# A gated pair of spectral filters: the first inverse step mostly without column tiles, rows of x and the last output row in smaller pieces

## The chip, the core and the metric

The kernel runs on one core of one Trainium2 chip. The metric is the device time of one launch in microseconds (us). Before the change the median of three runs is 131.76 us (131.26 to 131.91). One further execution was profiled, and the views below are of that one.

## What is computed

One input x of 2048 rows and 1024 columns goes through two filters in the frequency domain (a two-dimensional real transform, a product with complex weights, the inverse transform). A gate, one number per row of x, mixes the two results. Both filters get the same x, so the forward transform is made once. Only A_x is read; B_x is not used by the reference either.

```python
def _A_ref(x, w_r, w_i):            # _B_ref is the same function
    B, S, D = x.shape               # 1, 2048, 1024, bfloat16
    X = jnp.fft.rfft2(x.astype(jnp.float32), axes=(-2, -1))
    X = X * (w_r + 1j * w_i)        # weights (2048, 513)
    y = jnp.fft.irfft2(X, s=(S, D), axes=(-2, -1)).astype(jnp.bfloat16)
    return y

x = A_x
g = sigmoid((x * gate_w).sum(-1, keepdims=True))
a = _A_ref(x, A_w_r, A_w_i)
b = _B_ref(x, B_w_r, B_w_i)
return g * a + (1 - g) * b
```

## The kernel before

The transforms are matrix products. A row of the input has two numbers: its place p on the 128 partitions and n2, one of 16, so that n2 counts 16 "row blocks" of 128 rows. The stages, by the names of the planner's nodes:

- **x, F, W, DM, SK, DI, MS, RM**: loads on SP's queue. xload (line 544) brings two row blocks (512 KB) at a time, DEPTH and FP give the order of x and of the parts of the matrix F. W0 and W1 are the weights of the two filters, four times four parts each. DM is loaded a second time at the end with other contents (RM).
- **fS, fT** (lines 632, 633): VectorE folds two row blocks, sum and difference of each row with its mirror image; for block 14 another pair (u0, u1) follows. **S1**: eight matmuls for each row block; **Z**: its eviction from PSUM to R3.
- **gate, zrow, zg, zp**: four groups of matmuls with 32 columns of the array for each (line 616), for the gate's transform.
- **D, Q** and **S2, X** for 16 groups kg: the rest of the forward transform, eight 256-wide matmuls and two tiny ones, then four 512-wide ones, each with an eviction of 128 x 1024.
- **mul, sum** (prod, line 729): VectorE multiplies X with the weights of filter b, for the pair m of two groups kg, in two products of 2048 elements and two sums of 1024. The pairs in SPLIT leave the sums out, and the matmuls behind them have twice the terms ("wide").
- **I1, V, turn** (stage_i1, line 751): the first inverse step. For each filter b, pair m and half h, each matmul has 64 weight columns and writes 64 PSUM partitions; r = 0 and r = 1 sit beside each other in the array as two column tiles. So one group is eight matmuls (sixteen when wide), one eviction V of 128 x 1024 into a "ub" tile, and one transfer "turn" of 256 KB within the on-chip memory, from the 128 partitions of ub to 16 partitions of U, eight rows of 2 KB in each (lines 777 to 779). There are 32 such groups, 16 for each filter.
- **x5, p5m, p5a, v5, V5, v5t, U5**: the last frequency column, 512, by itself. **gm, sig, RA, RB**: the gate and its product with the second inverse matrix.
- **Sj0, Sj1, Sk1, T, Dinv, o** (inverse, line 854): for each row block the second inverse step, eight matmuls for each filter into one PSUM tile (Sk1, the one that needs U5, stands alone), an eviction T, eight matmuls Dinv and an eviction o. Block n2 needs all turns with h = n2 // 8. Then **h0, h1, y0, y1** on VectorE and the transfer **out**; two row blocks share these except the last two, 14 and 15, which have them alone.

The order within each engine is planned: TABLE holds, for each node in the order in which the program adds it, a letter for its engine (p TensorE, a ScalarE, v VectorE, s SP) and a number, its place. Plan.run (line 321) walks through the nodes as an event simulation with costs written by hand; on each engine, the node of lowest place that is ready and finds room in its tile pools goes next. The pools and their limits are in the Plan at line 481 ("ub": ten tiles between V and the landing of the turn). The result is a fixed instruction order for each engine, with semaphores. All helpers record at a few lines: L493 is every matmul, L496 every VectorE operation on two tensors, L518 an eviction by ScalarE, L519 an eviction by VectorE, L524 every transfer.

Of the kernel before, what the change touches and what calls it, by code (L numbers as in the profile page):

```python
# [9 lines left out]
ALU = mybir.AluOpType  # L10
AP = bass.AP
# [6 lines left out]
v80 a100 s90 s145 s200 s255 s310 s365 s420 s475 s530 s585 s640 s695 a240 s750 s805 s860 s915 s978 s1105 s1168 s1295  # L18
s1358 s1421 s1484 s1548 s1611 s1674 s1737 s1801 s1864 s1927 s1990 s2054 v90 p160 a612 p1815 a1862 v505 v444 p666
v774 p578 a712 v611 v672 p840 a953 p753 a861 v888 v948 p1022 a1130 p1109 a1222 v1088 v1028 p1284 a1405 p1197 a1313  # L20
v1305 v1244 p1378 a1496 p1466 a1588 v1379 v1439 p1640 a1771 p1553 a1679 v1513 v1573 p1728 a1869 p1839 v1947 v1708
v1648 v1782 v1855 p1970 a2039 p2070 a2135 p1926 a1991 p2058 p2014 v2091 p2166 p2114 v2199 p2288 p2245 a2321 p2393
v2426 p2508 v2532 s2109 s2172 s2298 s2362 s2488 s2551 s2615 s2678 s2741 s2804 s2868 s2931 s2994 s3057 s3121 s3184
p2300 a2414 p2523 a2631 p2414 a2529 p2703 v2810 v3052 v3226 v2939 v3166 p3501 a3636 s3745 p3328 a3453 s3562 p2610
a2724 p2883 a2995 p2789 a2904 p3062 a3178 v3288 v3515 v3401 v3575 p3767 a3910 s4020 p3681 a3819 s3928 p2969 a3087
p3242 a3361 p3149 a3270 p3415 a3544 v4096 v4270 v3983 v4210 p4477 a4642 s4752 p4387 a4551 s4660 p3587 a3727 p3853
a4002 p3940 a4093 p4206 a4368 v4792 v5019 v4905 v5079 p5372 a5509 s5618 p5192 a5326 s5435 p4294 a4459 p4569 v4678
p4660 a4774 p4933 a5051 v5487 v5714 v5600 v5774 p5897 a6009 s6119 p5983 a6101 s6210 p4840 a4960 p5106 a5234 p5278
a5417 p5551 a5692 v6062 v6235 v5948 v6175 p6737 a6870 s6979 p6478 a6595 s6705 p5458 a5600 p5724 v5834 p6069 a6192
p6391 a6504 v6870 v6997 v7057 v7184 p7353 a7466 s7575 p7439 a7557 s7666 p6184 a6298 p6650 a6778 p6298 a6412 p6564  # L30
a6687 v7258 v7372 p7698 a7892 s8001 p7526 a7719 s7829 v6984 p7168 v7245 v7833 v7846 v8467 v8477 v8533 v8520 v8559
# [14 lines left out]
QD = False  # L46
SPLIT = ((0, 7), (1, 6), (1, 7))
FULL = (14,)
DEPTH = tuple((i, i + 2) for i in range(0, 16, 2))
FP = ((0, 2), (2, 6), (6, 11), (11, 16))  # L50


# [888 lines left out]
```

## Time and profile before

| | us |
|---|---|
| median of the runs | 131.76 |
| the profiled execution | 131.37 |
| its span in the profile | 129.5 |
| TensorE busy | 117.5 |
| VectorE busy | 107.5 |
| ScalarE busy | 100.2 |

The span is the time from the first to the last instruction of the profiled execution; 1.9 us of its time lie outside. PE is TensorE's matmuls, PEld its weight loads, DVE VectorE, ACT ScalarE, SP the engine that issues transfers. A row of the table by stretch has the stretch, its length, then the busy time of each engine with the number of instructions, the granted clock of TensorE, the share of time in which the 16 DMA engines were busy, and the rate. A row of the timeline has the start, the length, the engine, the line and operation, output <- input with the names of the on-chip tensors (PS is PSUM, R the large buffers, RING the tile ring), the shape, how many were merged, and in brackets the idle time before and what ended it. "128*64 128x512" is a matmul with 128 rows and 64 columns of the array and 512 elements streamed. The ends of matmuls are modelled and overlap, so that their starts tell more than their busy time.

### The profile page before, as it was taken

The page shows a single profiled execution, that of the slowest core. Times are in us where ns is not written, and L with a number is a line of the kernel's source. Part 1 is how long each engine was busy: PE and PEld are TensorE (multiplying, and loading weights), DVE is VectorE, ACT ScalarE, POOL GpSimd, SP SyncE. Part 2 cuts the span into 40 slices and gives each one's busy share as a digit, 9 for nine tenths or more (in the row PEclk, how much of TensorE's full clock was granted, in tenths as well). Part 3 has the DMA queues.
Part 4 walks back from the last instruction along what each step waited for, and adds up shares of the span by engine and source line. Part 5 has one row for each costly group of instructions (what it writes and reads, how often), then busy time and mean ns, then how long its engine had stood idle before and what let it go on. Part 6 is the DMA issues. An engine that isn't in the chain of part 4 may idle for free.

```text
span 129.5 us, 2793 instructions
## 1 busy us (share of the span) xinstructions
PE 117.5 (91%) x1149; PEld 76.6 (59%) x1149; DVE 107.5 (83%) x155; ACT 100.2 (77%) x109; POOL 0.2 (0%) x4
## 2 busy tenths in 40 slices
PE   6687999899999999999999999999969999999710
PEld 2365786566544455445483555555659999999600
DVE  1386796417999997998899999998965899999992
ACT  4348898597999997999799958667335659999950
POOL 0000000000000000000000000000000000000000
PEclk9999999999999999999999999999999999999996
DMA  4999999999999997406348998987630004435474
GB/s 116 289 379 419 407 418 372 378 378 387 382 380 372 218 193 180 132 0 161 90 128 217 289 209 190 221 200 168 172 81 5 0 0 167 162 149 197 173 297 162
DMA packets 14064, 28.62 MB, mean 221 GB/s; under 512 B 1506, under 2 KB 5858, under 8 KB 14051
## 3 DMA queue, kind: packets, MB, share of 16 engines
q1 hardware_dynamic: 14048, 28.44, 70.2%
q8 instruction: 9, 0.15, 0.5%
q14 instruction: 5, 0.03, 0.1%
q10 hardware_dynamic: 2, 0.00, 0.0%
HBM read 15.85 MB, written 4.19 MB: 155 GB/s over the span
## 4 chain that ended last, share of the span: by engine, by line
PE 60%; DVE 20%; DMA 9%; issue 3%; SPq 3%; ACT 2%; DVEq 0%
PE PS L493 60%; DVE R L496 14%; DMA R<-in_A_x_dram 7%; DVE R L519 4%; SPq L524 3%; DMA R<-RING 3%; ACT R L518 2%; DVE RING L496 1%; DVE RING L519 1%; ACT RING L518 1%; DVEq L248 0%; DVE V L519 0%
## 5 line engine op out<-in xcount | busy, mean ns | idle before, releaser
L518 ACT ACTIVATE R<-PS 128x1024 bf16<-128x1024 f32 x52 | 50.9, 1028 | 12.9 <-PE PS L493 12.7
L518 ACT ACTIVATE RING<-PS 128x1024 bf16<-128x1024 f32 (+1 forms) x48 | 46.7, 1008 | 8.8 <-PE PS L493 8.8
L496 DVE TENSOR_TENSOR RING<-R 128x2048 bf16<-128x2048 bf16 (+1 forms) x48 | 47.8, 1043 | 6.2 <-DMA R<-in_A_x_dram 6.1
L493 PE MATMUL PS<-RING,SK 128*64 128x512 bf16 (+1 forms) x368 | 51.2, 382 | 0.1
L493 PEld LDWEIGHTS PS<-RING,SK 128*64 128x64 bf16 (+1 forms) x368 | 21.5, 108 | 24.3 <-issue 6.7
L493 PE MATMUL PS<-DM,R 128*128 128x256 bf16 (+1 forms) x256 | 27.4, 245 | 0.5 <-DMA R<-RING 0.5
L493 PEld LDWEIGHTS PS<-DM,R 128*128 128x128 bf16 x256 | 18.9, 97 | 5.7 <-issue 2.1
L519 DVE CAST R<-PS 128x1024 bf16<-128x1024 f32 (+1 forms) x16 | 15.2, 961 | 8.1 <-PE PS L493 8.1
L496 DVE TENSOR_TENSOR R<-R 128x1024 bf16<-128x1024 bf16 (+1 forms) x36 | 20.6, 626 | 0.3
L496 DVE TENSOR_TENSOR RING<-RING 128x1024 bf16<-128x1024 bf16 x28 | 18.2, 684 | 0.1
L493 PE MATMUL PS<-DI,R 128*128 128x256 bf16 x128 | 16.1, 273 | 1.3 <-ACT R L518 1.3
L493 PE MATMUL PS<-R,RING 128*128 128x256 bf16 (+1 forms) x128 | 14.5, 266 | 2.6 <-DVE RING L496 2.6
L493 PEld LDWEIGHTS PS<-R,RING 128*128 128x128 bf16 x128 | 11.4, 98 | 6.0 <-DVE RING L496 4.5
L493 PEld LDWEIGHTS PS<-DI,R 128*128 128x128 bf16 x128 | 11.7, 98 | 3.0 <-ACT R L518 1.6
L493 PE MATMUL PS<-RING,R 128*128 128x128 bf16 x128 | 9.3, 219 | 0.0
L493 PEld LDWEIGHTS PS<-RING,R 128*128 128x128 bf16 x128 | 7.7, 98 | 0.6 <-DVE R L519 0.4
L493 PE MATMUL PS<-MS,R 128*128 128x1 bf16 (+1 forms) x40 | 5.2, 165 | 0.0
L519 DVE CAST RING<-PS 128x512 bf16<-128x512 f32 (+1 forms) x4 | 3.8, 958 | 1.6 <-PE PS L493 1.5
L493 PE MATMUL PS<-RING 128*128 128x512 bf16 x8 | 3.5, 615 | 1.2 <-DVE RING L588 1.2
L493 PEld LDWEIGHTS PS<-MS,R 128*128 128x128 bf16 (+1 forms) x40 | 3.4, 96 | 0.4 <-issue 0.2
L844 ACT ACTIVATE RING<-PS 128x512 bf16<-128x512 f32 x4 | 2.4, 601 | 1.1 <-DVE RING L496 1.1
L493 PE MATMUL PS<-R,G 128*32 128x512 bf16 x32 | 2.5, 384 | 0.4 <-ACT R L518 0.4
(34 smaller groups left out, 17.7 us busy)
## 6 DMA issues: line engine op xcount, KB each, us to landing
R<-RING SPq DMA_DIRECT2D x32, 256.0 KB, 4.4
R<-in_A_x_dram SPq DMA_DIRECT2D x8, 512.0 KB, 8.3
out_dram<-R SPq DMA_DIRECT2D x7, 512.0 KB, 2.6
R<-in_A_w_r_dram SPq DMA_DIRECT2D x7, 256.5 KB, 9.6
R<-in_A_w_i_dram SPq DMA_DIRECT2D x7, 256.5 KB, 9.5
R<-in_B_w_i_dram SPq DMA_DIRECT2D x7, 256.5 KB, 8.1
R<-in_B_w_r_dram SPq DMA_DIRECT2D x7, 256.5 KB, 8.2
R<-c_F SPq DMA_DIRECT2D x2, 320.0 KB, 7.6
```

The source lines that it names most:

```text
L493: return lambda e: e.matmul(o, l, r, start=start, stop=stop, skip_group_check=True)
L496: return lambda e: e.tensor_tensor(out=o, in0=a, in1=b, op=op)
L518: return [lambda e: e.activation(o, i, ACT.Copy)]
L519: return [lambda e: e.tensor_copy(o, i)]
L524: lambda e: [lambda q, d=d, s=s: q.dma_start(d, s) for d, s in pairs()],
L844: P.add("sig", {"act": (0.5, 0.7)}, lambda e: [lambda e: e.activation(rg(gr, 0, [[1, 512]]), psl(t, 0, [[1, 512]]), ACT.Sigmoid)], [(t,)], ...
```

## The change

- Of the 16 pairs (b, m), all but (1,5), (1,6) and (1,7) lose the column tiles. Each r has a group of its own (I0): four matmuls (eight when wide) of 128 weight columns, which give both halves h for one group kg. Its eviction is 128 x 1024 as before, and it is turned by two transfers of 128 KB: 64 source partitions of ub to 8 partitions of U, for h = 0 and h = 1. The three tiled pairs keep one transfer for each h. Keys of U now count 16 groups kg instead of eight pairs.
- x is loaded as single row blocks for 0, 1, 14 and 15, with pairs between; F comes in three parts instead of four. The folds of blocks 0 to 3 and 14, 15 are made in single row blocks, four operations of 512 for two blocks instead of two of 1024.
- The warm-up has seven matmuls instead of eight.
- Sk1 is merged into Sj1 where n2 % 8 > 1.
- For the last row block, Dinv, eviction (oh), h0 and h1 are made in two halves (by parity of the column frequency), and the output goes out as two transfers of 128 KB, one behind y1 and one behind y0.
- The planner gets a cost for going into or out of a tiled shape on TensorE, other pool limits, a rate of 400 instead of 390 for x, and a new TABLE. By the new table the four gate groups stand together, the wide group of (1,7) is split by v5 and v5t, the gate mix (gm, sig, RA, RB) comes before the last V, and VectorE gets the evictions X1, Q7, V of (1,3) and V of (1,6) between 27 and 88 us of the table's places (before: X1, X8, X12 and both V of (1,4)).

The diff without the table:

```diff
@@ -15,39 +15,42 @@
 NW = 16 * NS
 CELL = 512
...
 QD = False
 SPLIT = ((0, 7), (1, 6), (1, 7))
+TILED = ((1, 5), (1, 6), (1, 7))
 FULL = (14,)
-DEPTH = tuple((i, i + 2) for i in range(0, 16, 2))
-FP = ((0, 2), (2, 6), (6, 11), (11, 16))
+DEPTH = ((0, 1), (1, 2)) + tuple((i, i + 2) for i in range(2, 14, 2)) + ((14, 15), (15, 16))
+FP = {1: (0, 4), 3: (4, 8), 5: (8, 16)}
...
+        self.switch = 0.11
...
+                    if e == "pe" and n.kind != kind:
+                        kind = n.kind
+                        occ, lat = occ + self.switch, lat + self.switch
                     n.eng, n.start = e, now
                     free[e] = now + occ
                     n.end = now + lat
@@ -479,9 +486,9 @@
     GW = R4
 
     P = Plan({"ps": 8, "ring": NCELL, "t": 32, "late": 32},
-             {"ps": ("ps", 4), "p1": ("ps", 8), "sj": ("ps", 3), "st": ("ring", 3), "u": ("ring", 1), "q": ("ring", 4),
-              "t": ("ring", 2), "tn": ("ring", 4), "pp": ("ring", 2), "g": ("ring", 1), "gz": ("ring", 1), "RA": ("ring", 1), "ub": ("ring", 10), "w": ("ring", 1), "T": ("t", 4),
-              "o": ("late", 2), "h": ("late", 2), "y": ("late", 3)})
+             {"ps": ("ps", 4), "p1": ("ps", 8), "sj": ("ps", 3), "st": ("ring", 3), "u": ("ring", 2), "q": ("ring", 3),
+              "t": ("ring", 2), "tn": ("ring", 4), "pp": ("ring", 4), "g": ("ring", 2), "gz": ("ring", 2), "RA": ("ring", 1), "ub": ("ring", 10), "w": ("ring", 1), "T": ("t", 3),
+              "o": ("late", 3), "h": ("late", 2), "y": ("late", 3), "yl": ("late", 2)})
     HOME = {"ring": RING, "t": R4, "late": R5}
     xv = A_x[0].rearrange("(p r) d -> p r d", r=16)
     outv = out[0].rearrange("(p r) d -> p r d", r=16)
@@ -503,7 +510,9 @@
         return {"dve": (0.07 + 0.00052 * n, 0.205 + 0.00052 * n)}
 
     def pe(name, ns, build, reads, writes, alloc=(), **kw):
-        return P.add(name, cost(ns), lambda e: build(), reads, writes, alloc=alloc, **kw)
+        n = P.add(name, cost(ns), lambda e: build(), reads, writes, alloc=alloc, **kw)
+        n.kind = {"I1": 1, "gate": 2}.get(name, 0)
+        return n
 
     def ev(name, n, io, reads, writes, slow=False, only=None, **kw):
         x = 0.285 if slow else 0.0
@@ -543,14 +552,12 @@
 
     def xload(a, b):
         dma("x", "sp", lambda: [(ap(R1, a * 1024, [[1024, b - a], [1, 1024]]), xv[:, a:b, :])],
-            (b - a) * 0.262, 390, [], [("x", i) for i in range(a, b)])
-
...
+    for i, (a, b) in enumerate(DEPTH):
+        if i in FP:
+            f0, f1 = FP[i]
+            cload("sp", R2, f0 * 256, "F", f0 * 256, f1 * 256, [("F", j) for j in range(f0, f1)])
         xload(a, b)
     dma("gw", "act", lambda: [(ap(GW, 0, [[1, 1024]], 0, 1), gate_w.rearrange("(o d) -> o d", o=1))], 0.002, 400, [], ["gw"])
     cload("sp", MS, 0, "MS", 0, 410, ["MS"])
@@ -588,7 +595,7 @@
     P.add("zero", {"dve": (0.6, 0.7)}, lambda e: [lambda e: e.memset(rg(warm, 0, [[1, 512]]), 0.0)],
           [], [(warm, 0, 1)], alloc=[warm])
     wps = Tile("p1", 1)
-    pe("warm", [512] * 16, lambda: [mm(psl(wps, 0, [[1, 512]]), rg(warm, 0, [[1, 128]]), rg(warm, 0, [[1, 512]]), True, True) for _ in range(8)],
+    pe("warm", [512] * 14, lambda: [mm(psl(wps, 0, [[1, 512]]), rg(warm, 0, [[1, 128]]), rg(warm, 0, [[1, 512]]), True, True) for _ in range(7)],
        [(warm, 0, 1)], [(wps,)], alloc=[wps])
 
     gp = Tile("p1", 1)
@@ -629,8 +636,15 @@
         lo = ap(R1, n2 * 1024, [[1024, 2], [512, 2], [1, 256]])
         hi = ap(R1, n2 * 1024 + 1023, [[1024, 2], [-512, 2], [-1, 256]])
         xs = [("x", n2), ("x", n2 + 1)]
-        P.add("fS", vt(1024), lambda e: [tt(rg(st, 0, [[1024, 2], [256, 2], [1, 256]]), lo, hi, ALU.add)], xs, [(st, 0, 1), (st, 2, 3)], alloc=[st])
-        P.add("fT", vt(1024), lambda e: [tt(rg(st, 512, [[1024, 2], [256, 2], [1, 256]]), lo, hi, ALU.subtract)], xs, [(st, 1, 2), (st, 3, 4)])
+        if n2 < 4 or n2 == 14:
+            for r in range(2):
+                for name, c, op in (("fS", 0, ALU.add), ("fT", 1, ALU.subtract)):
+                    P.add(name, vt(512), lambda e, r=r, c=c, op=op: [
+                        tt(rg(st, r * 1024 + c * 512, [[256, 2], [1, 256]]), ap(R1, (n2 + r) * 1024, [[512, 2], [1, 256]]),
+                           ap(R1, (n2 + r) * 1024 + 1023, [[-512, 2], [-1, 256]]), op)], xs[r:r + 1], [(st, 2 * r + c, 2 * r + c + 1)], alloc=[st])
+        else:
+            P.add("fS", vt(1024), lambda e: [tt(rg(st, 0, [[1024, 2], [256, 2], [1, 256]]), lo, hi, ALU.add)], xs, [(st, 0, 1), (st, 2, 3)], alloc=[st])
+            P.add("fT", vt(1024), lambda e: [tt(rg(st, 512, [[1024, 2], [256, 2], [1, 256]]), lo, hi, ALU.subtract)], xs, [(st, 1, 2), (st, 3, 4)])
         if n2 not in FULL:
             for r in range(2):
                 stage_s1(n2 + r, st, r)
@@ -752,31 +766,44 @@
         p = PT[b, m]
         T = UR[b]
         pt = pit[id(T)]
-        for h in range(2):
-            P.key = ("IA", "IB")[b], 2 * m + h
+        wide = isinstance(p, list)
+        terms = [(768, 0, 0), (1792, 0, 512), (1024, 1, 0), (1024, 1, 512)] if wide else [(768, 0, 0), (1024, 0, 512)]
+
+        def data(r, i):
+            return rg(p[terms[i][1]] if wide else p, r * 1024 + terms[i][2], [[1, 512]])
+
+        def matrix(r, i, o, w):
+            return ap(SK, terms[i][0] + (512 if r == m == 0 else 0) + o, [[1, w]])
+
+        def turn(u, kgs, h, p0, n, k):
+            dma("turn", "sp", lambda: [(AP(T, (64 * (kgs[0] % 2) + m) * pt + h * 8192, [[8 * pt, k], [1024, 8], [1, 1024]]), rg(u, 0, [[1, 1024]], p0, n))],
+                n / 128 * 0.262, 205, [(u, 0, 2)], [("U", b, kg, h) for kg in kgs], n=1.15, after=allz(h) if b else [("x", i) for i in range(16)])
+
+        if (b, m) in TILED:
+            for h in range(2):
+                P.key = ("IA", "IB")[b], 2 * m + h
+                t, u = Tile("ps", 2), Tile("ub", 2)
+
+                def halves(h=h, t=t):
+                    return [mm(psl(t, o * 512, [[1, 512]], 64 * r, 64), matrix(r, i, o * 128 + h * 64, 64), data(r, i), i == 0, i == len(terms) - 1)
+                            for o in range(2) for i in range(len(terms)) for r in range(2)]
+                keys = [(q, 0, 4) for q in p] if wide else [(p, i, i + 1) for i in range(4)]
+                pe("I1", [512] * 2 * len(terms), halves, keys + ["SK"], [(t,)])
+                ev("V", 1024, lambda t=t, u=u: (rg(u, 0, [[1, 1024]]), psl(t, 0, [[1, 1024]])), [(t,)], [(u, 0, 2)])
+                turn(u, (2 * m, 2 * m + 1), h, 0, 128, 16)
+            return
+        for r in range(2):
+            P.key = ("IA", "IB")[b], 2 * m + r
             t, u = Tile("ps", 2), Tile("ub", 2)
 
...
+            def whole(r=r, t=t):
+                return [mm(psl(t, o * 512, [[1, 512]]), matrix(r, i, o * 128, 128), data(r, i), i == 0, i == len(terms) - 1)
+                        for o in range(2) for i in range(len(terms))]
+            keys = [(q, 0, 4) for q in p] if wide else [(p, 2 * r, 2 * r + 1), (p, 2 * r + 1, 2 * r + 2)]
+            pe("I0", [512] * 2 * len(terms), whole, keys + ["SK"], [(t,)])
             ev("V", 1024, lambda t=t, u=u: (rg(u, 0, [[1, 1024]]), psl(t, 0, [[1, 1024]])), [(t,)], [(u, 0, 2)])
-            dma("turn", "sp", lambda u=u, h=h: [(AP(T, m * pt + h * 8192, [[8 * pt, 16], [1024, 8], [1, 1024]]), rg(u, 0, [[1, 1024]]))],
-                0.262, 205, [(u, 0, 2)], [("U", b, m, h)], n=1.15, after=allz(h) if b else [("x", i) for i in range(16)])
+            for h in range(2):
+                turn(u, (2 * m + r,), h, 64 * h, 64, 8)
 
     def x512():
         P.key = ("x5", 0)
@@ -818,7 +845,7 @@
         pe("v5t", [16] * 8, tr, [("V5", b), "MS"], [(t2,)])
         for h in range(2):
             ev("U5", 8, lambda h=h: (ap(UR[b], 512 + h * 8192, [[1024, 8]]), psl(t2, h * 8, [[1, 8]])), [(t2,)], [("U5", b, h)], only="dve",
-               after=[("U", b, m, h) for m in range(8)])
+               after=[("U", b, kg, h) for kg in range(16)])
 
     for kg in range(16):
         stage_d(kg)
@@ -851,8 +878,29 @@
     for c in range(4):
         gmix(c)
 
+    def finish(v, o, h):
+        for p in range(2):
+            P.key = ("E", 15)
+            t = Tile("p1", 1)
+            pe("Dinv", [256] * 4, lambda p=p, t=t: [
+                mm(psl(t, c * 256, [[1, 256]]), rg(v, (c * 4 + 2 * p + i) * 128, [[1, 128]]), ap(DI, ((2 * p + i) * 2 + c) * 256, [[1, 256]]), i == 0, i == 1)
+                for c in range(2) for i in range(2)], [(v, 0, 2), "DI"], [(t,)], alloc=[t] + ([] if p else [o]))
+            ev("oh", 512, lambda p=p, t=t: (rg(o, p * 512, [[1, 512]]), psl(t, 0, [[1, 512]])), [(t,)], [(o, p, p + 1)])
+            P.key = ("U", 15)
+            a, b = rg2(o, p * 512, [[1, 256]]), rg2(o, p * 512 + 256, [[1, 256]])
+            P.add("h0", vt(256), lambda e, p=p, a=a, b=b: [tt(rg(h, p * 512, [[1, 256]]), a(), b(), ALU.add)], [(o, p, p + 1)], [(h, p, p + 1)], alloc=[] if p else [h])
+            P.add("h1", vt(256), lambda e, p=p, a=a, b=b: [tt(rg(h, p * 512 + 511, [[-1, 256]]), a(), b(), ALU.subtract)], [(o, p, p + 1)], [(h, p, p + 1)])
+        for i, op in enumerate((ALU.add, ALU.subtract)):
+            y = Tile("yl", 1)
+            P.add("y%d" % i, vt(512), lambda e, y=y, i=i, op=op: [
+                tt(rg(y, 256 * i, [[256 - 512 * i, 2], [1, 256]]), rg(h, 0, [[256, 2], [1, 256]]), rg(h, 512, [[256, 2], [1, 256]]), op)],
+                [(h, 0, 1), (h, 1, 2)], [(y, 0, 1)], alloc=[y])
+            d = outv[:, 15, 256:768] if i else AP(outv.tensor, outv[:, 15, 0:256].offset, [list(outv[:, 15, 0:256].ap[0]), [768, 2], [1, 256]])
+            dma("out", "sp", lambda y=y, d=d: [(d, rg(y, 0, [[1, 512]]))], 0.131, 400, [(y, 0, 1)], [], kind="out", n=0.65)
+
     def inverse(ns):
         k = len(ns)
+        last = ns == (15,)
         o, h, y = Tile("o", 2 * k), Tile("h", 2 * k), Tile("y", 2 * k)
         for r, n2 in enumerate(ns):
             P.key = ("S", n2)
@@ -864,14 +912,19 @@
                            R(n2 * 128), b == 0 and j in (0, 4), b == 1 and j in (3, 4)) for j in js]
             for b in range(2):
                 g = ("RB", n2 // 4) if b else (RA, n2 // 4, n2 // 4 + 1)
-                u = [("U", b, m, n2 // 8) for m in range(8)]
+                u = [("U", b, kg, n2 // 8) for kg in range(16)]
                 if not b:
                     pe("Sj0", [128] * 8, lambda fns=fns: fns(0, range(8)), u + [("U5", 0, n2 // 8), g], [(t,)])
+                    continue
+                if n2 % 8 > 1:
+                    pe("Sj1", [128] * 8, lambda fns=fns: fns(1, (0, 1, 2, 3, 5, 6, 7, 4)), u + [("U5", 1, n2 // 8), g], [(t,)])
                     continue
                 pe("Sj1", [128] * 7, lambda fns=fns: fns(1, (0, 1, 2, 3, 5, 6, 7)), u + [g], [(t,)])
                 pe("Sk1", [128], lambda fns=fns: fns(1, (4,)), [("U5", 1, n2 // 8), g], [(t,)])
             ev("T", 1024, lambda t=t, v=v: (rg(v, 0, [[1, 1024]]), psl(t, 0, [[1, 1024]])), [(t,)], [(v, 0, 2)])
             P.key = ("E", n2)
+            if last:
+                break
 
             def inv(t=t2, v=v):
                 f = []
@@ -884,6 +937,8 @@
                 return f
             pe("Dinv", [256] * 8, inv, [(v, 0, 2), "DI"], [(t2,)], alloc=[t2] + ([o] if r == 0 else []))
             ev("o", 1024, lambda t=t2, r=r: (rg(o, r * 1024, [[1, 1024]]), psl(t, 0, [[1, 1024]])), [(t2,)], [(o, 2 * r, 2 * r + 2)])
+        if last:
+            return finish(v, o, h)
         d2 = [1024, k]
         P.key = ("U", ns[0])
         oc = [(o, 2 * r, 2 * r + 2) for r in range(k)]
```

## The prediction

> **What bounds the kernel now.** I read the busy time by stretch first.
>
> ```profile
> core 0: us, PE busy (x) PEld busy (x) DVE busy (x) ACT busy (x) POOL busy (x), PEclk, DMA share, GB/s
> 35.00:50.00 15.00, 15.00 (x119) 7.58 (x119) 14.11 (x17) 14.62 (x16) 0.00 (x0) 1.00 1.01 278
> 50.00:62.00 12.00, 12.00 (x92) 5.57 (x89) 11.16 (x13) 11.57 (x12) 0.00 (x0) 1.00 0.45 116
> 62.00:76.00 14.00, 14.00 (x121) 7.59 (x122) 13.86 (x16) 12.41 (x15) 0.00 (x0) 1.00 0.74 188
> 76.00:90.00 14.00, 14.00 (x135) 7.34 (x134) 13.54 (x25) 10.06 (x11) 0.00 (x0) 1.00 0.90 195
> ...
> 104.00:126.60 22.60, 18.94 (x246) 17.28 (x244) 22.36 (x37) 18.42 (x20) 0.00 (x0) 1.00 0.41 164
> ```
>
> From 35 to 90 us TensorE never rests, and VectorE has 55 - (14.11 + 11.16 + 13.86 + 13.54) = 2.3 us left; ScalarE has 6.3. From 104 us on VectorE is full. The chain that ended last agrees: it stays on TensorE from 27.01 for 62.93 us and from 103 us mostly on VectorE.
>
> So what TensorE does with its time between 35 and 92 us counts. The timeline shows it matmul by matmul:
>
> ```profile
> 49.30 0.49 PE L493 MATMUL PS<-DM,R 128*128 128x256 bf16 x3
> ...
> 50.32 1.05 PE L493 MATMUL PS<-RING,SK 128*64 128x512 bf16 x8
> 51.30 0.50 PE L493 MATMUL PS<-DM,R 128*128 128x256 bf16 x3
> ...
> 52.24 3.96 PE L493 MATMUL PS<-RING,SK 128*128 128x512 bf16 x24
> ```
>
> Starts are to be read, since the ends overlap. A D stage takes 52.24 - 51.30 = 0.94 us when an S2 follows and 51.30 - 50.32 = 0.98 is one I1 group of eight column-tiled matmuls (four pairs). The D stage before that group takes 50.32 - 49.30 = 1.02. Four full 512-wide matmuls (S2) take 0.87: their weights come at 48.42, the next D matmul at 49.30. So pairs of column tiles cost what full matmuls cost, plus 0.08 us on entering the tiled shape and 0.11 on leaving. The waits of weight loads show the same thing, as idle time that nothing releases:
>
> ```profile
> 46.58 1.44 PEld L493 LDWEIGHTS PS<-RING,SK 128*64 128x64 bf16 x16 [0.21 <-issue]
> 48.42 0.55 PEld L493 LDWEIGHTS PS<-RING,SK 128*128 128x128 bf16 x4 [0.41 <-issue]
> ```
>
> Here two groups take 48.42 - 46.58 = 1.84, eight pairs at 0.216 would be 1.73: 0.11 again, with the entry before it. I take 0.21 us for a visit to the tiled shape, in and out.
>
> **The change, part by part.** The profiled execution took 131.37 us, with a span of 129.5; the sum is made against it. The median of the runs shown is 131.76, so 0.39 is added at the end. From the table I use only each node's engine and the order.
>
> *Column tiles.* Before, TensorE goes into the tiled shape 16 times between 35 and 92 us. By the new order only (1,5), (1,6), (1,7) are tiled, in 4 visits. 12 x 0.21 = **-2.5 us** on the engine that sets this stretch (bounds -2.8, and -1 if the neighbours stop it). The work stays: half as many matmuls of full width, the same evictions.
>
> *What is late next there: VectorE.* It has 2.3 us free. Of 1024-wide evictions it gets four instead of five in this stretch, which frees 1.2 (1221 ns each); four gate-mix operations of 512 that came after the last first-step eviction now come ahead of it (0.42 each alone, but two in a row take 0.76 in the chain, so 0.34 to 0.35 apart: 1.4). So 2.3 + 1.2 - 1.4 = 2.1 against the 2.5 that TensorE gives up: VectorE becomes just as tight. **+0.4** (bounds 0 and 1.5). ScalarE takes one more eviction, 1.0 of its 6.3.
>
> *Turns in two transfers.* 32 transfers of 256 KB become 52 of 128 KB and 6 of 256. Issues on SP take 0.38 to 0.71 us each in the chain, some 0.57 with the pause; from the first half of (0,5) to the last transfer that the first Sj1 needs there are 32 halves, 4 whole and the reload of RM: 37 x 0.57 = 21 us, beside some 29 us of TensorE steps (12 narrow and 2 wide full groups, 6 tiled ones, D, S2, gm, v5, three Sj0, 8 shape changes). SP has room, and what waits behind a turn there is only other turns. The data itself: a whole turn runs at 195 GB/s in the row 76 to 90 above, where the DMA share is 0.90; 0.262 MB / 195 = 1.34 us. **A half is not in the trace.** From below it is 0.67; from above it is what a whole one takes, 1.34, if only half of the 16 DMA engines, or of what they meet in memory, serve it (64 source partitions and 8 destination partitions instead of 128 and 16). With 0.67 the stretch needs 32 x 0.67 + 4 x 1.34 + 1.3 = 28.1 us, plus some 2.5 from issue to landing for the last: 30.6 against 29. I charge **+0.9**, taking 0.67 to 0.70, because the only packets that a split adds are four-byte completions. Each 0.1 us more per half adds 3.2 us, as nothing else covers it: the ten ub tiles fill, then evictions wait, then TensorE.
>
> [...]
>
> *The opening.* Before:
>
> ```profile
> 4.33 1.29 DVE L496 TENSOR_TENSOR RING<-R 128x1024 bf16<-128x1024 bf16 x2 [3.18 <-DMA R<-in_A_x_dram]
> ...
> 5.68 1.81 PE L493 MATMUL PS<-R,RING 128*128 128x256 bf16 x15 [1.01 <-DVE RING L496]
> ```
>
> The first fold waits for two rows of x (512 KB) and lasts 1.29; now it waits for one row and two 512-wide operations (0.34 apart), so S1 starts about 1.1 us earlier. Later loads carry the same bytes, so the last row lands where it did, near 17.3 us; TensorE then has less backlog, but not 1.1 less. I take -0.6. The four gate rows stood apart, four visits to a tiled shape (32 columns); now they stand together, one visit: 3 x 0.2 = -0.6. Together **-1.2** (bounds -2.0, and 0 if the last fold, four operations 0.34 apart instead of two in 1.30, then the u pair, ends as late as before). One warm matmul less lies ahead of the first load's landing and costs nothing unless the full matmul rate, which the eight (3.47 us) bring, then comes later.
>
> *The tail.*
>
> ```profile
> 120.08 6.93 DVE L496 TENSOR_TENSOR R<-R 128x1024 bf16<-128x1024 bf16 x14
> ...
> 121.67 1.96 PE L493 MATMUL PS<-DI,R 128*128 128x256 bf16 x16 [0.69 <-ACT R L518]
> 122.05 5.32 SPq L524 DMA_DIRECT2D out_dram<-R  x4
> 122.75 1.94 ACT L518 ACTIVATE R<-PS 128x1024 bf16<-128x1024 f32 x2 [0.22 <-PE PS L493]
> ```
>
> From the end of the last Dinv (123.63) to the last issue's end (127.37) pass 3.7 us: an eviction of 1.03, four VectorE operations behind those of row 14, an issue. In halves it is an eviction of 0.60, h0 and h1 of 256 (between 0.17 and 0.42 each, say 0.27), y1 and y0 (0.34 apart), an issue: some 2.3. That is -1.4, if VectorE is free, which the row from 104 us denies: two more operations there cost 0.2, but it enters the tail without one eviction and four gate-mix operations (2.5 us), with one more eviction to do later. I take **-1.0** (bounds -2.0 and +0.3). The last transfer is 128 instead of 256 KB: below 0.2, left out. The merged Sj1 has the same eight matmuls; it may wait 0.2 for U5.
>
> Sum: -2.5 + 0.4 + 0.9 - 1.2 - 1.0 = -3.4. 131.37 - 3.4 = 128.0, and with 0.39 for the median **128.4 us**.
>
> **Rivals.** *VectorE takes over.* If it is full from 28 to 88 us and every wait now lands on the path, 1.5 instead of 0.4 is paid, and the opening gives nothing but the gates (-0.6): -1.7, 130.1 us. For it: 13.86 of 14 busy. Against it: full rows there show no idle time between operations.
>
> *The halves are slow; slower than before.* A half takes between 0.67 and 1.34 us; transfers become the bound from about 50 us. At 1.0: 32 x 0.33 = +10.6 on 128.4: 139.0. At 1.34: +21.4, and 4 for the twelve halves before: about 154. It decides from 0.67 + 3.4/32 = 0.78 us. For it: whole turns already run at half the rate of loads, and the DMA share is 0.90. Against it: whatever halves the rate of whole turns may be shared by all engines, and eight engines at the loads' pace would carry half of 390, 195 GB/s, which is 0.67.
>
> *The shape change is not what costs.* If the 0.1 us belonged to any change of operands, only opening and tail would remain: 131.76 - 2.2 + 0.9 = 130.5. Against it: S2 to D shows 0.22 from start to start, a plain step.
>
> **How the numbers follow.** Forecast 0.52 (own range 126.8 to 129.6); VectorE 0.07; shape 0.03; slow halves 0.38, of which 0.13 above 140. The range 126.8 to 140 leaves out this 0.13 and 0.05 below. A measurement tells about 0.5% (0.66 us) from no change: faster 0.57, same 0.05, slower 0.38, the same and the first points of slower coming from halves between 0.75 and 0.8.
>
> **What would show it.** Right: PEld idle "issue" falls by more than half, TensorE stays gapless from 27 to 88 us, and the first Sj waits under 1 us for a turn. Wrong: idle time of ScalarE or TensorE released by "DMA R<-RING", GB/s well under 195 in a stretch with the DMA share low and turns queued (slow halves); PE waiting for DVE RING (VectorE).

## The result and the profile after

The changed kernel takes **145.78 us** (median of 4 runs, 145.44 to 150.39) against 131.83 us of the kernel before in the same session: a ratio of 1.105 with a 95% interval of 1.099 to 1.111. The forecast of 128.4 us is wrong, the time lies above the range, and it went the way of the rival of slow halves. The profiled execution took 145.54 us with a span of 143.8. Some executions of most kernels here were disturbed and slower; medians are over all runs, ratios over the undisturbed ones alone.

Busy time by stretch, the kernel after:

```profile
core 0: us, PE busy (x) PEld busy (x) DVE busy (x) ACT busy (x) POOL busy (x), PEclk, DMA share, GB/s
35.00:50.00 15.00, 15.00 (x106) 9.15 (x104) 15.00 (x18) 14.43 (x17) 0.00 (x0) 1.00 0.80 262
50.00:62.00 12.00, 9.54 (x57) 4.33 (x55) 11.91 (x15) 9.38 (x11) 0.00 (x0) 1.00 0.49 113
62.00:76.00 14.00, 11.16 (x66) 5.01 (x64) 7.74 (x9) 10.76 (x13) 0.00 (x0) 1.00 0.60 140
76.00:90.00 14.00, 12.53 (x62) 4.79 (x60) 10.59 (x12) 9.69 (x11) 0.00 (x0) 0.88 0.57 145
```

To 50 us it looks as forecast: TensorE without a gap. Then TensorE and ScalarE have idle time, from 62 us on VectorE too, while the transfers move 113 to 145 GB/s at a DMA share of 0.49 to 0.60: the sign that the prediction had named for slow halves. The chain that ended last now runs through the turns (R<-RING) for 27% of the span, where the kernel before had 3%:

```profile
PE PS L500 28%; DMA R<-RING 27%; ACT RING L527 10%; SPq L533 7%; DMA R<-in_A_x_dram 7%; DVE R L503 6%; ACT R L527 5%; DVE R L528 2%; DVE RING L503 1%; DVE DM L503 0%; DVEq L265 0%; DVE RING L528 0%; ACT Q L527 0%; DVE P L503 0%; DVEq L251 0%
```

The waits of the whole span (who waits, for whom; us in total, times, longest) tell more:

```profile
PEld PS L500 <- ACT RING L527: 13.7, 20, 2.4
DVE RING L503 <- DMA R<-RING: 10.4, 4, 4.5
ACT RING L527 <- DMA R<-RING: 9.8, 8, 2.4
PEld PS L500 <- issue: 8.1, 20, 2.4
```

ScalarE and VectorE wait for turns (R<-RING) until cells of the ring are free, TensorE waits for ScalarE. Before, no engine waited for R<-RING for as much as 1 us. The landing times in the trace give the pace of halves that stand in the queue, and the records of the packets show what is slow; the second row is of a run told below:

```
                               landings one after the other, us               2-KB packets, 54 to 60 us
after (8 apart)     55.74 56.91 58.13 59.28 60.51 61.56 62.73: 1.17 each      320, median 167 ns
e5_ports (4 apart)  71.84 72.50 73.16 73.83 74.49 75.15 75.81: 0.66 each      469, median  84 ns
```

These are stretches where the queue never empties. Over the whole trace, halves that were issued well (1.2 us or more) before the one ahead of them landed came 1.16 us apart in the median and 1.09 in the mean; in e5_ports 0.67 and 0.82. A half leaves 9 updates of its semaphore where a whole turn leaves 16: one first, then eight when the data land, and between 54 and 60 us 8 packets are in flight in the median, though other halves stand in the queue: read here as 8 engines for a half, and the same for the next. A packet of 2 KB takes 84 ns at full pace (the median of the 401 from 5 to 17 us, all of them loads); in this stretch most take twice that.

The opening, TensorE in the kernel after, and below it the granted clock of one stretch:

```profile
5.93 1.03 PE L500 MATMUL PS<-R,RING 128*128 128x256 bf16 x8 [1.55 <-DMA R<-c_F]
7.46 1.49 PE L500 MATMUL PS<-R,RING 128*128 128x256 bf16 x8 [0.49 <-DVE RING L503]
9.10 2.99 PE L500 MATMUL PS<-R,RING 128*128 128x256 bf16 x16 [0.15 <-DVE RING L503]
```

```profile
core 0: us, PE busy (x), PEclk, DMA share, GB/s
8.00:9.00 1.00, 0.95 (x5) 0.50 0.95 250
```

S1 starts 0.25 us later than before (5.93 for 5.68), because the first piece of F, not the fold, comes last (the fold was done at 4.15); then the granted clock is 0.50 for some 3.4 us. The first S2 starts at 27.42 instead of 27.01.

The tail, after:

```profile
135.26 6.04 DVE L503 TENSOR_TENSOR R<-R 128x1024 bf16<-128x1024 bf16 x15
...
135.98 5.85 SPq L533 DMA_DIRECT2D out_dram<-R  x5
137.59 1.05 PE L500 MATMUL PS<-DI,R 128*128 128x256 bf16 x8 [1.12 <-ACT R L527]
```

From the last Dinv's end (138.64) to the last issue's end (135.98 + 5.85 = 141.83) pass 3.2 us, for 3.7 before. VectorE runs fifteen operations without a break until 141.30.

### The profile page after: what moved, and what is told of

Read it like the earlier page. It is cut to its first block, busy times and chain, and to the rows that moved or that the text cites. A ratio compares the mean times of both kernels' runs of the same rounds, so it can differ in the third digit from the quotient of the medians.

```text
span 143.8 us, 2613 instructions
## 1 busy us (share of the span) xinstructions
PE 120.8 (84%) x1036; PEld 76.7 (53%) x1036; DVE 107.3 (75%) x162; ACT 100.4 (70%) x111; POOL 0.2 (0%) x4
## 4 chain that ended last, share of the span: by engine, by line
DMA 34%; PE 28%; ACT 15%; DVE 10%; SPq 7%; issue 4%; DVEq 0%; ACTq 0%
PE PS L500 28%; DMA R<-RING 27%; ACT RING L527 10%; SPq L533 7%; DMA R<-in_A_x_dram 7%; DVE R L503 6%; ACT R L527 5%; DVE R L528 2%; DVE RING L503 1%; DVE DM L503 0%; DVEq L265 0%; DVE RING L528 0%; ACT Q L527 0%; DVE P L503 0%; DVEq L251 0%
## 5 line engine op out<-in xcount | busy, mean ns | idle before, releaser
L527 ACT ACTIVATE R<-PS 128x1024 bf16<-128x1024 f32 (+1 forms) x55 | 53.7, 1021 | 15.2 <-PE PS L500 14.7
L503 DVE TENSOR_TENSOR RING<-R 128x2048 bf16<-128x2048 bf16 (+2 forms) x54 | 48.5, 945 | 19.2 <-DMA R<-RING 8.2
L500 PE MATMUL PS<-RING,SK 128*128 128x512 bf16 (+1 forms) x256 | 54.4, 401 | 5.4 <-ACT RING L527 3.6
L527 ACT ACTIVATE RING<-PS 128x1024 bf16<-128x1024 f32 (+1 forms) x46 | 45.7, 1043 | 17.5 <-DMA R<-RING 9.8
L500 PEld LDWEIGHTS PS<-RING,SK 128*128 128x128 bf16 (+1 forms) x256 | 20.4, 105 | 32.0 <-ACT RING L527 7.9
L503 DVE TENSOR_TENSOR R<-R 128x1024 bf16<-128x1024 bf16 (+2 forms) x38 | 20.7, 602 | 0.3
L528 DVE CAST R<-PS 128x1024 bf16<-128x1024 f32 (+1 forms) x14 | 12.8, 924 | 8.9 <-PE PS L500 5.2
L500 PE MATMUL PS<-R,RING 128*128 128x256 bf16 (+1 forms) x128 | 15.7, 283 | 3.1 <-DMA R<-c_F 1.6
L528 DVE CAST RING<-PS 128x512 bf16<-128x512 f32 (+1 forms) x6 | 5.7, 951 | 1.0 <-PE PS L500 1.0
L503 DVE TENSOR_TENSOR RING<-DM,RING 128x512 bf16<-128x512 bf16 x4 | 1.6, 412 | 2.2 <-DMA R<-RING 2.2
```

Of the source, the lines that this page charges most:

```text
L500: return lambda e: e.matmul(o, l, r, start=start, stop=stop, skip_group_check=True)
L503: return lambda e: e.tensor_tensor(out=o, in0=a, in1=b, op=op)
L527: return [lambda e: e.activation(o, i, ACT.Copy)]
L528: return [lambda e: e.tensor_copy(o, i)]
```

## The experiments

Theory at the start: a half has only 8 of the 16 DMA engines (8 packets in flight, a DMA share of 0.49 from 50 to 62 us), and these are the bound. Rivals: the number of transfers with their issues; the memory that they read and write. The planner works out the order anew for each kernel. Where the order on TensorE, VectorE and ScalarE is that of the kernel compared with, a run is called clean; the others are told last. All ratios are to the kernel before.

**Half turns from GpSimd** (e1_pool, clean).

```
-            dma("turn", "sp", ...
+            dma("turn", "sp" if n == 128 else "pool", ...
```

> The changed kernel, with its 52 half turns issued by GpSimd instead of SyncE; the six whole turns stay on SyncE. Theory (engines): a half is served by 8 of the 16 DMA engines, the same 8 each time when SyncE issues it, and these 8 are the bound at about 1.13 us per half (landings 52 to 68 us). If halves issued by GpSimd fall on other engines in turn, two of them run side by side, landings come 0.6 to 0.75 us apart, and the time falls to 127 to 131 us. If GpSimd's halves use the same 8 engines, nothing changes: 145 to 147. Rival (memory): 64 source partitions and 8 destination partitions limit the rate, whatever engines move the data: landings stay 1.1 apart, 145 to 147. Second rival (issue): a GpSimd issue takes over 1.2 us, then the landings follow the issues and the time is 146 or more. [...]

141.1 us, ratio 1.070 (1.066 to 1.075). Now 10 packets of turns are in flight in the median from 54 to 60 us and 16 from 66 to 70, where the changed kernel has 8, and 30 us of SyncE's issues (52 of 0.59) have gone elsewhere, but a turn still takes long to land. The DMA issues on its page:

```profile
R<-RING POOLq DMA_DIRECT2D x52, 128.0 KB, 5.1
```

Its packets are 4 KB; between 54 and 60 us their median is 282 ns, where such a packet alone takes 159 (so in e11_ports_pool below). More engines meet the same obstacle: the theory of the engines explains at most a third of the loss.

**The whole turn of the kernel before, cut in two** by columns (e3_cols, 16 engines, 1 KB a row) and by partitions (e4_parts, the shape of the halves). Both clean.

```
+ [(... + q, [[8 * pt, 16], [1024, 8], [1, 512]]), rg(u, q, [[1, 512]])) for q in (0, 512)]          e3_cols
+ [(AP(T, (64 * r + m) * pt + ..., [[8 * pt, 8], ...]), rg(u, 0, [[1, 1024]], 64 * r, 64)) for r in range(2)]   e4_parts
```

> The kernel before, column tiles and all, with each whole turn cut into two transfers by columns: 128 source partitions and 16 destination partitions each, 512 elements (1 KB) a row, 64 transfers of 128 KB in all. Theory (engines): each still has 16 engines, 128 KB takes 0.65 to 0.85 us, and the time is that of the kernel before or up to 3 us more: 131.5 to 135 us. Rival (count): each transfer of 128 KB costs what a half costs in the changed kernel, 1.1 us, whatever its shape: 64 of them need 70 us instead of 43, and the time is 145 to 160 us.

> The kernel before, column tiles and all, with each whole turn cut into two transfers by partitions: 64 source partitions and 8 destination partitions each, rows of 2 KB as before, 64 transfers of 128 KB, the shape that the changed kernel's halves have. Theory (engines) and the memory rival alike: 1.1 us each, 64 need 70 us from about 47 us on, so the first Sj comes near 118 to 122 instead of 92 us and the time is 152 to 162 us. If halves were slow in the changed kernel for another reason (its order, its places, its longer runs of matmuls), this one is near the kernel before: 131.5 to 135 us.

By columns 133.47 us, ratio 1.012 (1.007 to 1.017): 64 transfers instead of 32 cost 1.6 us, so their number is not what costs 14. By partitions 138.78 and 142.45 us in two runs, below the 152 to 162 of both theories and above the 131.5 to 135 of the other case. The profile is of the slower run. Its packets are fast at times (median 84 ns from 78 to 96 us, at 188 GB/s and a DMA share of 0.52) and slow at others (140 ns from 66 to 78). So 8 engines can carry a half in 0.66 us (pairs land 1.26 to 1.34 us apart from 88 to 96 us), as the forecast had it. Something else doubles the packets: in e4_parts one half after the other writes to the other 64 partitions, in the changed kernel two halves in a row write to the same eight.

The new theory: what counts is which partitions are written. The eight destination partitions of a half stand 8 apart (m, m + 8, ..., m + 56). That this spacing is what doubles the packets was the author's conjecture; 4 apart, with all else the same, is its test.

**Destination partitions 4 apart** (e5_ports, clean; the same order on every engine).

```
- AP(T, (64 * (kgs[0] % 2) + m) * pt + h * 8192, [[8 * pt, k], [1024, 8], [1, 1024]])
+ AP(T, (64 * (m // 4) + 32 * (kgs[0] % 2) + m % 4) * pt + h * 8192, [[4 * pt, k], [1024, 8], [1, 1024]])
...
+ (RM, MS and the windows of v5t permuted alike)
```

> The changed kernel with one thing moved: where the rows of the first inverse step's result lie in its partitions. The 8 destination partitions of a half stand 4 apart instead of 8 apart (the constants that are indexed by this partition are permuted alike). Same transfers, same 8 engines, same issues. The packets of 2 KB show two durations, about 84 ns alone and about 165 ns; in the changed kernel their median is 167 between 54 and 60 us. [...] Then with partitions 4 apart the median is 84 to 100 ns, halves land 0.65 to 0.8 us apart, the waits for R<-RING nearly go, and the time is 127 to 132 us. Rival (engines): 8 engines carry a half in 1.0 to 1.15 us wherever it goes: 144 to 147 us. [...]

**133.0 us** (12 runs), ratio 1.004 (1.001 to 1.008): 0.101 of 131.8, some 13.3 us, are gone, with the same transfers, engines and issues. Its stretches, and the wait that is left between 27 and 97 us:

```profile
50.00:62.00 12.00, 11.63 (x70) 5.42 (x70) 11.77 (x15) 11.60 (x14) 0.00 (x0) 1.00 0.46 146
62.00:76.00 14.00, 12.37 (x74) 5.43 (x76) 11.76 (x14) 12.21 (x15) 0.00 (x0) 1.00 0.55 174
```

```profile
ACT RING L527 <- DMA R<-RING: 2.3, 3, 1.3
```

The DMA share is nearly that of the kernel after (0.46 for 0.49), but it moves 146 GB/s instead of 113. Halves land 0.66 us apart, the packets' median is 84 ns. The spacing is shown to be the cause. How it acts is not shown: the runs give the packets' two durations, 167 and 84 ns, and not what makes them wait.

**The controls** (both clean): two halves by partitions in the kernel before, 4 apart (e6_parts_ports), and the kernel before with nothing but the spacing (e7_before_ports).

```
+ AP(T, (64 * (m // 4) + 32 * r + m % 4) * pt + h * 8192, [[4 * pt, 8], ...]) for r in range(2)    e6_parts_ports
+ AP(T, (64 * (m // 4) + m % 4) * pt + h * 8192, [[4 * pt, 16], ...])                          e7_before_ports
```

> The kernel before with each whole turn cut in two by partitions, as in the earlier run of that kind (140.6 us), and with destination partitions 4 apart. [...] Rival (engines): as the earlier run, 138 to 143 us.

> The kernel before with destination partitions 4 apart instead of 8 apart and nothing else. A whole turn then writes 16 partitions, 4 apart, instead of 16, 8 apart. [...]

e6_parts_ports: 136.31 us (three of four runs at 136.0 to 136.4), above the 131 to 134.5 that were expected if the spacing is all that counts, and below the rival's range. It is 2.5 less than the faster run 8 apart, with a median of 84 ns throughout, yet 2.8 more than two transfers by columns. The rate is not why: queued pairs land some 1.3 us apart in both. That it is the 8 engines in another way is possible; the cause is open. e7_before_ports: 131.79, ratio 1.000 (0.997 to 1.003): whole turns don't care; the time of the kernel before, 131.0 to 132.5, was what had been expected.

**GpSimd once more, partitions 4 apart** (e11_ports_pool, clean against e5_ports). From SyncE a half has 8 engines and lands 0.66 us after the one before, as in e5_ports.

> The changed kernel with destination partitions 4 apart, its loads unchanged, and the half turns issued by GpSimd. [...] If that is still a bound, halves on engines in turn land 0.35 to 0.5 us apart where they are queued and the time is 0.5 to 2 us below the 132.2 us of SyncE's: 130.2 to 131.7. Rival: transfers are no longer the bound and GpSimd's longer way from issue to landing costs as much: 132 to 134 us.

133.3 us, ratio 1.000 (0.995 to 1.005), against 1.004 (1.001 to 1.008) from SyncE: by the two intervals a gain of up to 1.6 us is possible, and none. So relieving the 8 engines and SyncE's issues together gives back at most 1.6 of the 2.8 us (0.996 here below, 0.974 forecast) that are still missing once the loads are mended too; GpSimd's own way from issue to landing (2.6 us at the least) is part of that exchange.

**The opening's loads** (e9_loads, clean against e5_ports), then **the eighth warm matmul** on top (e10_warm8).

```
+ DEPTH = tuple((i, i + 2) for i in range(0, 16, 2))
+ FP = {1: (0, 2), 2: (2, 6), 3: (6, 11), 4: (11, 16)}
```

> The changed kernel with destination partitions 4 apart (as in the run that did this alone, 132.2 us over its undisturbed runs) and with the loads of x and F in the pieces and the order of the kernel before: x two rows at a time, F in pieces of 2, 4, 5 and 5 rows instead of 4, 4 and 8. The folds of single rows stay. Theory (loads): the opening lost its gain because the first piece of F, 256 KB, landed at 5.79 us instead of 128 KB at 4.79, and the second was as slow, so that x ended at 19.11 instead of 17.34 us and TensorE rested 1.55 us and ran at half its clock from 8 to 11.4 us. Then here S1 starts near 5.1 us, x ends near 17.3, S2 starts 1 to 1.8 us earlier than 27.27, and the time is 130.2 to 131.3 us. Rival: the backlog of VectorE and ScalarE sets the start of S2, whatever the loads: 131.8 to 132.8 us.

> The same as the run with the loads of the kernel before, and the eighth warm matmul put back. Forecast's term: it costs and brings nothing, within 0.3 us of that run. If the clock falls to half in the opening without it, 0.4 to 1.2 us faster than that run.

e9_loads: 131.91 us, ratio 0.996 (0.992 to 1.000), some 1.1 us below e5_ports. Its opening:

```profile
5.40 1.92 PE L500 MATMUL PS<-R,RING 128*128 128x256 bf16 x16 [1.02 <-DVE RING L503]
```

The fold ends the wait again, the clock stays at 1.00, S2 starts at 25.99 (25.88 and 26.60 in the two runs that follow). That the loads were late is no accident of one run: in the six profiles with the changed loads the first piece of F landed at 5.66 to 6.26 us and the last row of x at 18.83 to 19.14; in the thirteen with the loads of before at 4.74 to 5.00 and 17.31 to 18.26. e10_warm8: 131.6, ratio 0.9955 (0.992 to 0.999): the eighth matmul brings nothing, as forecast. That is 0.45% less than the kernel before.

**The tail in one piece** on e9_loads (e12_notail; clean but for the last row).

```
-        last = ns == (15,)
+        last = False
```

> The same as the run with the loads of the kernel before, and the last row's tail in one piece again, as before the change. Forecast's term: the halves are worth 1.0 us, bounds 2.0 and -0.3. The changed kernel's trace has 5.2 us from the end of the last Dinv to the span's end, the kernel before 5.9: by that 0.7. So 0.5 to 1.1 us slower than that run.

132.07 us against 131.91, ratio 0.992 (0.986 to 0.997) against 0.996 (0.992 to 1.000): no gain of the halves can be seen, and the 0.5 to 1.1 us that were expected are not there.

**Runs that tell little, since their order changed.** Issuing every second half from ScalarE (e2_act: 157.05), all pairs in tiles again (e8_tiled: 134.86), halves split between SyncE and GpSimd (e13_two_queues: 132.21), one transfer per full group (e14_one: 138.18), the same with GpSimd for every second (e15_one_two: 144.27), the products of six of the sixteen pairs left out in the mended kernel and in the one before (e16_light: 138.62, e17_before_light: 138.43), F in other pieces (e18_pieces: 139.16).

> The changed kernel, with the second half (rows 8 to 15) of each of its 26 split pairs of halves issued by ScalarE, the first by SyncE. Theory (engines): both queues feed the same 8 engines, so nothing is gained: landings of all halves still 1.0 to 1.15 us apart on the average, 145 to 149 us (ScalarE loses the issues' time). Rival (queue or count): what costs is that one queue handles one transfer after the other, at 0.59 us an issue on SyncE and some fixed time per transfer; then two queues overlap, landings come 0.7 apart and the time falls to 130 to 138 us.

> The changed kernel with all 16 pairs of the first inverse step in column tiles and whole turns, as before the change (the places of the full groups are given to the tiled ones). What is left of the change is the opening, the tail, the limits of buffers and the order. By the forecast's terms: opening -1.2 and tail -1.0, so 129 to 130 us. By my reading of the changed kernel's trace, where the opening came out 0.4 us later and the last row some 0.7 us shorter: 131 to 132.5 us.

> Base: destination partitions 4 apart, the loads of the kernel before, eight warm matmuls (0.9955 of the kernel before, its profiled run 130.53). Here the second half (rows 8 to 15) of each split pair is issued by GpSimd, the first by SyncE. Where the gain of the column tiles went: S2 starts 1.3 us earlier than before (25.70 for 27.01), but the last turn lands 1.0 us later (97.65 for 96.60), and SyncE issues half turns without a pause for most of the time from 75 us on, 0.65 to 0.76 us each. Theory S (SyncE's issues bound that stretch): relieved here, the last turn lands 1 to 2.5 us earlier and the time is 0.5 to 2 us below the base: 129 to 130.8. Theory G (8 engines at 0.66 us per half bound it): relieved here too if GpSimd's halves take other engines: the same times. Rival V (VectorE and ScalarE bound it): no gain, 131 to 132.5.

> The same base, with the columns of the first inverse step's matrix ordered so that one transfer of 256 KB carries a whole full group (128 source partitions, 8 destination partitions with 16 rows each, 8 engines), all 16 pairs of groups full, none in column tiles: 32 transfers, all issued by SyncE. SyncE's issues fall from 58 to 32; the 8 engines still need 16 x 0.084 = 1.34 us for each. Theory S: 0.5 to 2 us below the base, 129 to 130.8. Theory G: no gain from fewer issues, 130.8 to 132.5. Rival V: no gain, 131 to 132.5.

> The run with one transfer per full group, with every second one issued by GpSimd. Both bounds of the transfers are relieved, issues and engines. Theories S and G: 128.5 to 130.5. Rival V: as the base, 131 to 132.5; and if GpSimd's longer way to landing (2.6 to 3.1 us at the least) counts, up to 133.

> Base: destination partitions 4 apart, loads of the kernel before, eight warm matmuls (131.3 us over its undisturbed runs). Left out: the products of six of the sixteen pairs (pairs 1, 3 and 5 of both matrices take their neighbour's), 12 multiplications of 2048 and 12 sums of 1024, some 20 us of VectorE's work of which two thirds lie between 35 and 90 us; TensorE, ScalarE and the transfers keep all of theirs. Theory V: VectorE, through its products and evictions, is what held the column tiles' gain back: 127 to 129 us, the forecast's time. Rival (TensorE's order, ScalarE's evictions): 130.3 to 131.5 us.

> The kernel before with the products of the same six pairs left out. Theory (TensorE is the bound from 27 to 90 us in the kernel before, with its column tiles): nearly nothing is gained, 130.8 to 131.8 us, so the pair of light kernels stands 2 to 4 us apart, which is the column tiles' price with the opening's and the tail's gains. Rival (VectorE was as much the bound before): 128 to 130 us.

> Base: destination partitions 4 apart, eight warm matmuls. x is loaded as in the changed kernel (rows 0, 1, 14 and 15 alone), F in pieces of 2, 4 and 10 rows, each issued ahead of the second, third and fifth piece of x. Theory (loads): what was late in the changed kernel's opening was the first piece of F, of 4 rows; with 2 rows it lands before 4.6 us, S1 starts near 4.6 to 4.9 instead of 5.40 with the loads of the kernel before, and the time is 130.3 to 131.3. Rival (small pieces): the first row of x alone delays all that follows, x ends after 18.2 us, and the time is 131.5 to 133.

In all of them the planner, fed with other nodes or queues, put the steps of TensorE and VectorE in another order. That less work for VectorE made both kernels over 6 us slower shows how much such an order is worth, and that these times can't be charged to the edit. What does not depend on the order: in e14_one the queued groups land about 1.31 us apart (from 82.83 to 88.08 us, four intervals), as 16 packets of 84 ns on each of 8 engines must (1.34); and in e18_pieces a first piece of F of two rows lands at 4.02 us, but x ends at 18.50.

## Why the prediction was wrong, step by step

*Turns in two transfers: the step that failed.* It took 0.67 to 0.70 us for a half, and its working said that each 0.1 us more costs 3.2 us. Queued halves landed 1.17 us apart from 55 to 63 us. The bill agrees: the spacing alone took 13.3 us away, which is 0.42 us a half at that price, 1.09 in the mean, as in the landings. (Two stretches of 3.4 us at a granted clock of 0.50, from 76.2 and 103.5 us, which e5_ports doesn't have, are part of that bill.) So the rival had the mechanism and a price between its two (139.0 and 154). The reason against the rival, eight engines at the loads' pace give 0.67, was true (before, the loads move 372 to 419 GB/s from 6.5 to 42 us; e5_ports lands a half in 0.66), but it left open whether the eight could keep that pace wherever they write. The prediction counted only engines for the half. The 8 engines are there (9 updates, 8 packets in flight), but e5_ports has them too: by themselves they weren't what cost the 13 us. The step that the working lacked: write down the eight partition numbers (m, m + 8, ..., m + 56) and ask whether their spacing sets the pace. Why a whole turn runs at half the loads' rate, which the prediction left open, the runs don't show either: with 16 packets in flight (before, 80 to 88 us) a 2-KB packet takes 154 ns, with 8 in flight to partitions 4 apart (e14_one, 82 to 88 us) 84 ns, and both land 256 KB in about 1.3 us; 4 apart changes nothing for whole turns on 16 (e7_before_ports, 1.000). A smaller point: the working's own sum was 30.6 against 29 us, 1.6, and it charged 0.9.

*Column tiles: right on the single step, not in the time.* In the kernel after, TensorE between 43 and 54 us:

```profile
43.55 1.03 PE L500 MATMUL PS<-RING,SK 128*128 128x512 bf16 x4
44.41 0.49 PE L500 MATMUL PS<-DM,R 128*128 128x256 bf16 x3
...
48.85 4.50 PE L500 MATMUL PS<-RING,SK 128*128 128x512 bf16 x20
53.18 0.17 PE L500 MATMUL PS<-ZG,MS 128*128 128x16 bf16 x1
```

Four full matmuls take 44.41 - 43.55 = 0.86, five groups in a row (53.18 - 48.85) / 5 = 0.87; a tiled group took 0.98 and made the D stage ahead of it longer. The visits to the tiled shape between the first S2 and the first Sj fall from 16 to 4. But with the spacing and the loads mended, e9_loads still needs 66.5 us for that stretch where the kernel before needs 65.2, with TensorE idle 2.43 us instead of 0.07. By the prediction's terms (-2.5, +0.4, +0.9) it would need 64.0, so by these two profiles most of the 2.8 us that are missing are here. Its waits between 27 and 97 us:

```profile
PEld PS L500 <- ACT RING L527: 8.9, 20, 1.6
...
PE PS L500 <- DMA DM<-c_RM: 1.1, 1, 1.1
...
PEld PS L500 <- issue: 0.8, 2, 0.4
```

*What is late next: mis-sized, and other waits than VectorE's.* Before, the same view has 9.6 us of "issue" and 0.3 us of waits for ScalarE's ring evictions. These are waits of weight loads, of which matmuls still running hide the larger part. Of the 2.43 us that TensorE itself rests, two waits for ScalarE's ring evictions are 0.97, and one wait of 1.09 is for the reload RM, a wait for which the sum has no term. By the new order the first gm matmul, RM's first user, comes at 69 us, where RM has just landed (69.03); before it came at 84.64, long after the landing (74.70). The other runs with the changed kernel's order rest at this same matmul, 1.0 to 2.2 us. The step had +0.4 with 1.5 as the upper bound, and looked at VectorE's total instead of who delivers the next PSUM buffer and the next matrix. Argued, not shown: a ScalarE eviction lasts 1.02 us, a full group only 0.87, so where VectorE is in its products, groups in a row outrun the evictions; a tiled group at 0.98 did not. The runs that should have told this apart changed their order; some 2.8 us between e9_loads and the forecast stay open for that reason.

*Opening: nothing gained.* Forecast -1.2, +0.4 in the two profiles (27.42 for 27.01). The sign is not shown, since S2 starts at 27.01 to 27.93 in five profiles of the kernel before and its variants (before, e3, e4, e6, e7) and at 27.17 to 27.46 in the six with the changed loads. With the old loads and the rest of the change it starts at 25.88 to 26.75 (seven profiles), 1.3 earlier in the mean than those five, so the folds by rows and the gates in one visit together gave about what was forecast, and the new pieces of F and x took it back. "Later loads carry the same bytes, so the last row lands where it did" is the sentence that failed: it landed at 19.11 instead of 17.34. The half clock of the changed kernel's opening is not what cost: e11_ports_pool has the same loads, a full clock there and S2 at 27.43. The warm matmul's term was right: S1 begins at full rate (0.11 us from matmul to matmul, not 0.21) in 5 of 8 profiles with seven of them and in 8 of 12 with eight. In the kernel before, the eight (512 wide) start 0.43 us apart and S1's (256 wide) behind them 0.11, twice the rate; in the 4 of 12 the full rate came later, so the eight don't bring it every time.

*Tail: mis-sized.* Forecast -1.0; the stretch from the last Dinv's end to the last issue's end fell by 0.55, that to the span's end by 0.8 (5.9 to 5.1 us), and undoing the halves gives back 0.2 of it (5.3 in e12_notail). VectorE is full there, as the row from 104 us had said; two more operations stand in the same queue.

## What to carry to other kernels

Before a copy within the core's memory is cut, write down the partitions that each piece reads and writes, and try another spacing of them; a piece with half the bytes can take nearly the time of the whole (here 1.17 us for 128 KB, about 1.3 for 256, and 0.66 for 128 with the other spacing). A bound that is taken from one transfer holds for that shape alone, and "the same bytes" is no price for loads in other pieces. When TensorE's step gets shorter, compare it with the eviction that frees its next buffer, not with the evicting engine's total (this is argued here, not shown), and ask of each load whether its first user now comes sooner than it lands.

## What the hardware showed that was not expected

Queued copies of 128 KB on 8 engines landed every 1.17 us with their eight destination partitions 8 apart and every 0.66 us with them 4 apart (in the stretches shown); a 2-KB packet took 167 and 84 ns. F in 256 KB pieces (2 KB of each 8-KB row) ahead of single rows of x made the first piece land about 1 us later and the last row of x about 1.4 us later than the same bytes in other pieces; why, no run tells. In the changed kernel's opening TensorE's granted clock was 0.50 from 7.9 to 11.3 us after rests of 1.55 and 0.49 us with 1.03 us of work between them; in e11_ports_pool it stayed at 1.00 after rests of 1.51 and 0.52. And e7_before_ports, whose opening is that of the kernel before, ran its first matmuls 0.21 us apart, half the rate, until 10.46 us, where the kernel before had the full rate from 5.68. So the same opening can meet either clock; what decides, no run here shows.
